# A gated mix of a state-space layer and a linear attention on one core: the last two output blocks scaled in halves on two engines, and the order of all steps written anew

## The chip, the cores and the metric

The kernel runs on one core of a Trainium2 chip. The metric is the device time of one execution in microseconds (us). The kernel before took 155.13 us, the median of three runs (154.61 to 155.14).

## The reference, cut to what matters

```
g = sigmoid((x * gate_w).sum(-1))                 # x: 2048 x 512, bf16
a = 2 * Re(C h_t) + x * Dskip,  h_t = Lam_bar * h_(t-1) + B_bar x_t     # 512 complex states
q, k, v = x @ wqkv in 32 heads of 16;  pq = q @ w_phi, pk = k @ w_phi
phi(p) = concat(softmax(p), softmax(-p));  kv = sum_s phi(pk) v^T;  z = sum_s phi(pk)
b = (phi(pq) kv / (phi(pq) z + 1e-6)) @ wo
out = g * a + (1 - g) * b
```

## The kernel before, in words

The 2048 rows are dealt into 8 residues of 256 rows; a block is 128 rows of one residue, so there are 16 blocks. Everything lies in on-chip memory; eight PSUM banks take the results of the matmuls. Each piece of work is a Python generator whose `yield`s cut it into segments. One long string, `ORDER`, is an order written out by hand or by a planner: each token runs the next segment of a step, and the instructions of each engine keep this order (a manual schedule), so the string alone decides who stands behind whom on TensorE, VectorE, ScalarE and on SyncE's DMA queue. In a token, `@5` gives the PSUM banks that a segment takes, `:D` sends an evacuation to VectorE (ScalarE otherwise) and `:A` sends an output DMA to ScalarE's queue (SyncE's otherwise).

The steps that the change and the prediction touch:

- `W`, `f`: the key weights are transposed and folded with `w_phi`. `l8` to `l15` load a block of x transposed (`xT`, L229; blocks 0 to 7 are loaded ahead of the list); `NR` and `NI` load B (L284); `R` transposes B by DMA into `BT` (L288); `C`, `Q` and `J` do likewise for C and the query weights.
- `k`, `v`, `q` (L475): four 128x512 matmuls per block and an evacuation. `V` and `V2` turn small vectors through TensorE. `P`, `U`, `M`, `D`, `i`: the tables of the state-space layer; `M` runs on GpSimd.
- `x`, `n`, `e`, `s` with a number: max, min, exponential and normalisation of the keys' features of one group; `xA` to `sA`, and `X1` to `S3`, the same for the queries' groups of four blocks. The last VectorE segment of `sA` and of `S1` to `S3` is the multiplication L559; behind it four DMA transposes write `phT` (L563).
- `a` (L578): accumulation of kv. `g` (L601): B x, and `z`: the scan over time. `h` (L668): states of the other residues; for five residues VectorE adds the two parts (L672). `c`: scaling of C.
- For block n: `y` (L717, L722) is the state-space output, accumulated in a bank `py`; `o` takes `phT` to `pn` (L736), then `ld` and `rd` on ScalarE, `nu` on either engine, `on` on VectorE (L744), and the transposed `oT`, by DMA (L758), or through TensorE for blocks 12 to 15 (L753); `t` adds `oT @ Wo` to `py` (L765), scales by the gate into `ot` (L769 on ScalarE, L771 on VectorE) and stores it (L773).

In the evacuation of `pn`, ScalarE reads the sums (`ld`) and one of the engines the rest (`nu`) of the same PSUM tile:

```python
            aexp(out=ld[:, hf], in_=pn[:, :, Dh], func=ACT.Ln)
            evac(nu[:, hf], pn[:, :, 0:Dh])
```

Of the kernel before, what the change touches and what calls it, by code (L numbers as in the profile page):

```python
# [23 lines left out]
ORDER = """
NR F:28 NI B W1@0 W0@1 W0 W2@2 W1:D W3@3 W3 f1@4 W2:D f0@5 f2@6 f0 f1:D l10 V@0 F:4 V P f3@1 f3 f2:D F:4 P P k1@2 k1
l13 P2 k0@3 P2 U P2 P2 P2 P2 P4 k2@4 P3 P3 k3@5 P4 P4 k0 v0@0 i0 i2 U i0 i0 i1 i2 k4@7 i0:D i0 k2 i2 i2:D i2 U k3 k5@6
i1 v3@1 n0 x0 l9 i1 V2@2 i3 l12 x0 k4 v2@3 i3 i3 l14 i1 k5 n0 x0 n0 x0 i3 k7@4 n0 x0 U n0 i1 l11 k6@5 n1 x1 x1 n1 x1
n1 l8 R0 R1 x1 i3 k7 M v7@7 x1 n1 n1 k6:D L V2 v1@6 x2 n2 e0 v6@4 v5@5 v4@2 e0 x2 s0 v0 l15 n2 s0 n2 v2 s0 v1 R2 s0 v6
v3 n2 k10@0 k10 s0 k9@3 k9 C4 k13@6 gw D R3 s0 k12@4 e1 v7 s0 e1 s1 C6 k11@1 k11 x2 s1 k14@0 k8@3 k12 k14 k8 v4 k13
a0@71 a0 x2 s1 x2 s1 v5 g00@4 g00 g60@0 n2 x3 s1 g20@3 g60 s1 g10@2 g10 n3 e2 g30@6 g40@5 g10 s1 a1 x3 g20 n3 a1 x3 n3  # L30
x3 g41@4 n3 C3 e2 e2 e2 x3 g30 g40 g30 k15@0 k15 n3 e3 s2 x4 s2 x4 g01@2 g01 e3 e3 s2 g50@3 g11@5 g50 s2 s2 s2 n4 x4
n4 Q3 n4 s2 g50 g21@6 e3 s3 v8@0 g31@2 g11 Q2 g11 n4 g70@3 Q1 s3 C7 g21 g70 v9@5 g70 g70 z0 z0 g31 g31 Q0 w1@6 C0 a2
a2 a2 w0@3 s3 z0 v11@2 v9 g61@5 g41 R4 z0 w1 v8 z0 z0 g61 s3 w2@4 s3 s3 a2 x4 z0 z0 g51@6 g51 x4 w2 C2 s3 w3@0 g51 v11
n4 R5 w3 g71@5 g71 g71 g71 z1 z1 g02@4 g02 g42@6 a3 a3 z0 z0 g42 w0 e4 e4 z1 z1 z1 g62@2 g12@0 q1@5 C1 h50@4 C5 J1 e4
e4 z1 q2@6 q2 g12 g12 g22@3 g22 J0 h50 z1 z1 g62 q3@4 q3 J2 s4 z1 s4 q0@6 z1 s4 q0 q1 xA nA g32@0 J3 g32 g32 h60@3 J0
g52@2 g52 c4 h60 J2 c4 g52 h51@4 c2 s4 s4 g72@6 R7 g72 xA h10@5 nA g72 g72 c2 xA J3 nA h10 v10@0 v10 J1 s4 c5 h51 c5
R6 g23@3 v12@2 c4 c0 c0 g63@5 nA z2 z2 a3 a3 g03@4 xA g03 z2 z2 z2 z2 xA g23 z2 z2 g33@6 c5 v12 z2 z2 g13@0 g13 g63
g43@4 h32@3 g13 nA g43 h52@2 h52 g33 h32 h61@5 h61 h12@0 c0 g53@4 h12 g33 g53 s4 v14@3 c2 eA eA h42@2 h42 g73@6 g53 eA
eA g73 g73 q10@5 sA h11@0 h11 O h00@4 g73 sA v13@2 h00 v13 a4 z3 sA v15@6 z3 v15 h20@0 h01@4 h30@2 v14 h20 sA h30 z3
h31@6 z3 z3 sA a4 h01 h31 c6 c6 sA q13@3 q13 z3 a4 a4 Y Y h22@0 G q10 z3 z3 G q6@2 q6 h22 z3 z3 sA sA Y Y c1 c1 q9@4  # L40
q8@6 q5@7 h62@3 h41@5 c3 h41 c1 c3 c3 h13@0 h62 q11@2 h13 q11 q8 q12@1 c6 q12 h21@5 q5 h21 h02@2 c7 q4@6 q4 h53@3 h53
h23@1 h23 h33@0 h33 sA q9 h40@7 h40 sA q7@5 h43@6 h63@3 c7 h43 q7 c7 y4@0 y4 sA h63 sA h03@1 END h02 o0@4 o0 X1 N1
o1@7 o1 q14@6 X1 N1 h03 o0@5 X1 o1@2 o1 o1 o0 o0 q15@3 o2@4 o2 o2@7 o2 N1 q15 X1 N1 X1 N1 E1 E1 y2@1 y1@2 y1 E1 E1 q14
X2 y0@5 y0 o1 y4 X2 N2 X2 o0 o0 o3@4 o3 o3@7 o3 o1 o3 y2 X2 N2 o2 X2 N2 S1 S1 N2 S1 o3 S1 N2 S1 S1 o3 y5@3 o2 o2 S1 S1
S1 y1 E2 E2 E2 E2 y9@6 G N3 y5 y5 y3@4 y2 X3 X3 N3 t1 G t1 N3 S1 N3 S2 y9 y9 S2 S2 S1 S1 S2 y3 y3 t3 y0 t0 t0 t2 t2
y6@7 X3 t2:A o4@2 o4 o4@5 o4 o4 y6 y6 t3 X3 o4 X3 o4 S2 S2 t3 o5@1 o5 o5@2 o5 o5 y13@5 y13 o5 N3 o6@4 S2 o6 o6@1 o6 o6
y12@2 o5 y7@4 y7 y12 o6 o6 t4 y7 S2 S2 t4:D S2 E3 E3 E3 E3 S2 o7@1 o7 t5 t5 S3 o7@0 o7 S3 o7 t6 S3 o7 S2 o7 y8@1 o8@3
t6 o8 o8@0 o8 o8 S3 S3 y12 t0:A y11@7 o8 o8 o9@3 o9:D o9@0 o9:D S3 y8 y8 o9 o9 S3 S3 o9 o10@3 y11 o10 o10@0 y11 o10
o10 S3 y14@3 S3 y14 t7 t7:D t8 y14 t8 y15@0 o11@4 S3 o11 o11@1 t9 o12@4 o11:D o11 S3 o10 o10 o12 o12@1 o12 o12 t9:D
o11 y15 o13@4 o13:D o13@6 t6:A o13 o13 o11 o12 y10@1 o14@4 y15 o14:D o12@6 t9 o12:D t7:A t1 y10 y10 o13 o15@4 o15  # L50
o15@6 t4:A t5 o15 o15 t8 o15 t12 t12 t12:A t10 o14@4 o14 o14 t10:D o13@6 t11 o15@2 o15 t10 o13:D t11 t11:A y13 t13 o14
o14@1 t15 t15 t15 o14:D t14 t13 t13 t14 t14:A
"""
# [15 lines left out]
def kernel(  # L69
# [691 lines left out]
    def st_t(n):  # L761
        ti = order[n]
        py, oT = live["py", n], live["oT", n]
        for g in range(HG):
            MM(out=py[:], lhsT=oT[:, g, :], rhs=Wo[:, g, :], start=False, stop=(g == HG - 1))  # L765
        yield
        ot = pools["op"][1].tile([P, D], BF16, name="ot", bufs=14)
        if sel["eng"] == "act":
            nc.scalar.mul(out=ot[:], in_=py[:], mul=G[:, ti:ti + 1])  # L769
        else:  # L770
            VS(out=ot[:], in0=py[:], scalar1=G[:, ti:ti + 1], scalar2=None, op0=ALU.mult)  # L771
# [76 lines left out]
```

## Time and profile before

| | |
|---|---|
| three runs | 154.61, 155.14, 155.13 us; median 155.13 |
| the profiled execution | 155.28 us, of which its span is 153.2 |
| busy in the span | TensorE 146.2 (95%), VectorE 132.4 (86%), ScalarE 129.2 (84%), GpSimd 15.8 us |
| granted TensorE clock | 0.995 |
| transfers | 17.55 MB by DMA, mean 115 GB/s |

The span runs from the first to the last instruction; 2.1 us lie around it. Durations of single instructions overlap on an engine, so sums of durations are larger than busy times.

### The profile page before, as it was taken

The numbers are of one execution on the slowest core, as the hardware profiler recorded it, in microseconds if no ns is written. First come the engines' busy times: TensorE is split into PE (matmuls) and PEld (weight loads), VectorE is DVE, ScalarE is ACT, GpSimd is POOL, SyncE is SP. The second block draws the span as 40 slices with busy tenths as digits, with TensorE's granted clock in tenths as the row PEclk, the third lists the DMA queues.
The fourth block names the chain that finished last, engine by engine and source line by source line (L and its number), as shares of the span: only waits on it lengthen the run. The fifth ranks groups of instructions, "written<-read, shape, count | busy, mean of one in ns | idle before, by whom it ended". The sixth has DMA issues, their size and how long they took to land.

```text
span 153.2 us, 3361 instructions
## 1 busy us (share of the span) xinstructions
PE 146.2 (95%) x1236; PEld 95.0 (62%) x1254; DVE 132.4 (86%) x303; ACT 129.2 (84%) x279; POOL 15.8 (10%) x43
## 2 busy tenths in 40 slices
PE   7899999999999999999999999999999999999990
PEld 7644434788878985869867656555554455555540
DVE  3799999999999999999999999999999958717520
ACT  3489998999998999999998999699498998627562
POOL 8239980000000000000000000000000000000000
PEclk9999999999999999999999999999999999999997
DMA  4875995534445699930000007711278859969842
GB/s 116 164 218 97 223 178 112 103 75 103 103 107 78 129 230 178 166 115 4 0 0 4 0 0 169 74 37 34 42 98 147 176 122 189 162 129 206 247 143 103
DMA packets 50848, 17.55 MB, mean 115 GB/s; under 512 B 44176, under 2 KB 50832, under 8 KB 50832
## 3 DMA queue, kind: packets, MB, share of 16 engines
q1 hardware_dynamic: 48976, 15.75, 53.8%
q10 hardware_dynamic: 1696, 1.57, 3.2%
q8 instruction: 10, 0.16, 0.5%
q0 software_dynamic: 160, 0.01, 0.2%
q14 instruction: 6, 0.05, 0.1%
HBM read 2.64 MB, written 2.10 MB: 31 GB/s over the span
## 4 chain that ended last, share of the span: by engine, by line
PE 78%; SPq 10%; DMA 7%; issue 1%; ACT 1%
PE pgq L601 18%; PE py L717 16%; PE pq L475 9%; PE py L765 8%; SPq L229 8%; PE pv L475 4%; PE ph L668 4%; PE pk L475 4%; DMA xT<-in_A_x_dram 4%; PE kvacc L578 3%; DMA phT<-EEq 3%; PE pn L736 3%; PE pgq L606 2%; PE py L722 2%; PE pgq L608 2%; SPq L284 1%
## 5 line engine op out<-in xcount | busy, mean ns | idle before, releaser
L601 PE MATMUL pgq<-xT,BT 128*128 128x256 bf16 x256 | 31.5, 272 | 0.0
L475 PEld LDWEIGHTS <-xT 128*128 128x128 bf16 x192 | 18.2, 98 | 18.3 <-DMA xT<-in_A_x_dram 0.7
L601 PEld LDWEIGHTS <-BT 128*128 128x128 bf16 x256 | 24.6, 98 | 4.1
L138 ACT ACTIVATE EEk<-EEk 128x1024 bf16<-128x1024 bf16 x20 | 20.4, 1080 | 0.0
L119 ACT CAST uv<-pgq 128x512 bf16<-128x512 f32 x28 | 15.9, 605 | 0.5 <-PE pgq L601 0.4
L475 PE MATMUL pv<-Wv,xT 128*128 128x512 bf16 x59 | 15.5, 379 | 0.3
L475 PE MATMUL pq<-Wq,xT 128*128 128x512 bf16 x60 | 15.4, 379 | 0.2
L765 PE MATMUL py<-Wo,oT 128*128 128x512 bf16 x62 | 15.3, 379 | 0.1
L475 PE MATMUL pk<-Wk,xT 128*128 128x512 bf16 x62 | 14.7, 379 | 0.3 <-DMA xT<-in_A_x_dram 0.2
L138 ACT ACTIVATE EEq<-EEq 128x1024 bf16<-128x1024 bf16 x12 | 11.7, 1042 | 0.3 <-DVE EEq L527 0.3
L769 ACT ACTIVATE ot<-py,G 128x512 bf16<-128x512 f32 x12 | 7.9, 686 | 4.5 <-PE py L765 4.3
L138 ACT ACTIVATE ld<-pn 128x16 f32<-128x16 f32 x32 | 6.1, 191 | 5.7 <-PE pn L736 4.6
L590 ACT ACTIVATE phT<-X,dgB 128x512 bf16<-128x512 bf16 x16 | 10.7, 725 | 0.0
L119 ACT CAST nu<-pn 128x256 bf16<-128x256 f32 x27 | 9.9, 380 | 0.0
L119 ACT CAST vx<-pv 128x512 bf16<-128x512 f32 x16 | 9.1, 604 | 0.4 <-PE pv L475 0.4
L548 DVE TENSOR_TENSOR EEk<-EEk,rck 128x4096 bf16<-128x4096 bf16 (+1 forms) x5 | 9.3, 1858 | 0.0
L744 DVE TENSOR_TENSOR on<-nu,rd 128x512 bf16<-128x512 bf16 x16 | 6.7, 421 | 2.8 <-ACT rd L138 1.6
L765 PEld LDWEIGHTS <-oT 128*128 128x128 bf16 x64 | 5.7, 97 | 5.3 <-DMA oT<-on 0.5
L119 ACT CAST Xq<-pq 128x512 bf16<-128x512 f32 x16 | 8.9, 608 | 0.0
L119 ACT CAST Xq<-pk 128x512 bf16<-128x512 f32 x15 | 8.6, 598 | 0.4 <-PE pk L475 0.4
L736 PEld LDWEIGHTS <-phT 128*128 128x128 bf16 x128 | 6.2, 97 | 3.8 <-DMA phT<-EEq 1.4
L511 DVE TENSOR_TENSOR smk<-smk 128x512 bf16<-128x512 bf16 (+4 forms) x18 | 8.1, 448 | 0.1
(178 smaller groups left out, 321.2 us busy)
## 6 DMA issues: line engine op xcount, KB each, us to landing
X<-HM SPq DMA_DIRECT2D x8, 256.0 KB, 4.5
out_dram<-ot ACTq DMA_DIRECT2D x8, 128.0 KB, 2.5
out_dram<-ot SPq DMA_DIRECT2D x8, 128.0 KB, 2.2
C2r<-in_B_wqkv_dram ACTq DMA_DIRECT2D x2, 256.0 KB, 3.8
Wv<-in_B_wqkv_dram SPq DMA_DIRECT2D x1, 512.0 KB, 4.0
Bn<-in_A_B_re_dram SPq DMA_DIRECT2D x1, 512.0 KB, 5.7
Bn<-in_A_B_im_dram SPq DMA_DIRECT2D x1, 512.0 KB, 6.8
Wo<-in_B_wo_dram SPq DMA_DIRECT2D x1, 512.0 KB, 4.3
```

The source lines that it names most:

```text
L119: nc.scalar.copy(out=out_ap, in_=in_ap)
L138: ins = nc.scalar.activation(**kw)
L229: nc.sync.dma_start_transpose(out=xT[:, :, ti * P:(ti + 1) * P], in_=x_res[ti // 2, ti % 2])
L475: MM(out=pt[:], lhsT=xT[:, kt, ti * P:(ti + 1) * P], rhs=W[:, kt, :], start=(kt == 0), stop=(kt == KT - 1))
L511: VT(out=dst, in0=cur[:, :, :, 0:n, :], in1=cur[:, :, :, n:2 * n, :], op=op)
L548: VT(out=E5, in0=E5, in1=rc.to_broadcast([P, L, 2 * NB, Dh, 4]), op=ALU.mult)
L590: nc.scalar.mul(out=t_, in_=x_, mul=c_)
L601: MM(out=pg[:, h, :], lhsT=BT[:, kt, 2 * j + h, :], rhs=xT[:, kt, r * NC:(r + 1) * NC], start=(h == 0 and kt == 0), stop=(r % 2 == 0 and k ...
L717: MM(out=py[:], lhsT=hs(r, t, slice(a * P, (a + 1) * P)), rhs=C2B[t], start=(t == 0), stop=False)
L736: MM(out=pn[:, 4 * m:4 * m + 4, :].rearrange("p h e -> p (h e)"), lhsT=ph[:, 4 * hf + m, :], rhs=KVm[:, 4 * hf + m, :], start=(m == 0), st ...
L765: MM(out=py[:], lhsT=oT[:, g, :], rhs=Wo[:, g, :], start=False, stop=(g == HG - 1))
L769: nc.scalar.mul(out=ot[:], in_=py[:], mul=G[:, ti:ti + 1])
```

## The change

In `st_t` the last two blocks of the order of outputs (n = 14 and 15) are no longer scaled by one instruction over 512 columns. ScalarE scales columns 0 to 255 and VectorE columns 256 to 511, of the same PSUM tile `py` into the same tile `ot`; one DMA stores both. The string `ORDER` is replaced as a whole. It has the same 855 tokens; their order, the banks and the letters for engines and queues differ. The diff, with the ORDER lines that the prediction speaks of:

```diff
 ORDER = """
-NR F:28 NI B W1@0 W0@1 W0 W2@2 W1:D W3@3 W3 f1@4 W2:D f0@5 f2@6 f0 f1:D l10 V@0 F:4 V P f3@1 f3 f2:D F:4 P P k1@2 k1
-l13 P2 k0@3 P2 U P2 P2 P2 P2 P4 k2@4 P3 P3 k3@5 P4 P4 k0 v0@0 i0 i2 U i0 i0 i1 i2 k4@7 i0:D i0 k2 i2 i2:D i2 U k3 k5@6
-i1 v3@1 n0 x0 l9 i1 V2@2 i3 l12 x0 k4 v2@3 i3 i3 l14 i1 k5 n0 x0 n0 x0 i3 k7@4 n0 x0 U n0 i1 l11 k6@5 n1 x1 x1 n1 x1
-n1 l8 R0 R1 x1 i3 k7 M v7@7 x1 n1 n1 k6:D L V2 v1@6 x2 n2 e0 v6@4 v5@5 v4@2 e0 x2 s0 v0 l15 n2 s0 n2 v2 s0 v1 R2 s0 v6
...
-o11 y15 o13@4 o13:D o13@6 t6:A o13 o13 o11 o12 y10@1 o14@4 y15 o14:D o12@6 t9 o12:D t7:A t1 y10 y10 o13 o15@4 o15
-o15@6 t4:A t5 o15 o15 t8 o15 t12 t12 t12:A t10 o14@4 o14 o14 t10:D o13@6 t11 o15@2 o15 t10 o13:D t11 t11:A y13 t13 o14
-o14@1 t15 t15 t15 o14:D t14 t13 t13 t14 t14:A
+NR l8 B F:28 W1@0 NI W1 W0@1 W2@2 W2:D W3@3 l13 f1@4 W0 f0@5 W3 f0 f2@6 f1:D V@0 V l9 f2:D F:4 P P f3@2 U P2 f3 U P P2
+P2 P2 U P2 P4 P4 F:4 U k0@1 k0 V2@3 P3 k3@4 V2 P2 P3 k1@0 P4 k1 k2@5 i0 i1 i0 i0 i0 k2 i0 i1 v2@7 i2 i2 i2 k3 n0 x0 gw
+x0 n0 k4@6 i2 k4 x0 i1 i1:D i3 i3 k5@2 k5 n0 i3 x0 n0 v4@1 x0 l11 i3:D v3@3 n0 x1 n1 v6@0 l14 M x1 i1 i2 i3 L n1 x1 n1
+x1 n1 k7@5 x1 l10 l12 n1 k6@4 k6:D v5@6 k7 n2 x2 e0 e0 v0@2 v0 s0 s0 x2 s0 R0 n2 v2 v6 v1@5 v1 e1 k8@4 x2 k8 s0 s0 n2
+v7@2 v7 D v3 k13@7 k13 s0 e1 s0 R1 k9@0 v5 s1 n2 R3 s1 k14@5 k14 k11@4 k11 k10@2 k10 x2 C7 k12@3 k9 l15 R2 k12 C3 v4
...
+q11@7 q11 G q8 h22 h41@0 h43@3 h41 q14@4 sA sA h03 h20@2 h43 q14 h20 c7 sA sA h63@7 h63 END X1 N1 X1 o0@0 o0 q15@6 q15
...
+t12:D o15 o15 o15 o14@6 o14 t1 o14 t10 t10 o14 o13@2 t10:A t11 o15@6 o15 t12 o13:D o14@3 t13 t11 t11 y15 t15 y14 t13
+o14:D t15 t13:A t15 t14 t14 t14
 """
...
         ot = pools["op"][1].tile([P, D], BF16, name="ot", bufs=14)
-        if sel["eng"] == "act":
+        if n >= NTI - 2:
+            nc.scalar.mul(out=ot[:, 0:D // 2], in_=py[:, 0:D // 2], mul=G[:, ti:ti + 1])
+            VS(out=ot[:, D // 2:D], in0=py[:, D // 2:D], scalar1=G[:, ti:ti + 1], scalar2=None, op0=ALU.mult)
+        elif sel["eng"] == "act":
             nc.scalar.mul(out=ot[:], in_=py[:], mul=G[:, ti:ti + 1])
```

More of the change, by code (lines that the diff above doesn't have):

```diff
@@ L24 @@
 ORDER = """
-NR F:28 NI B W1@0 W0@1 W0 W2@2 W1:D W3@3 W3 f1@4 W2:D f0@5 f2@6 f0 f1:D l10 V@0 F:4 V P f3@1 f3 f2:D F:4 P P k1@2 k1
-l13 P2 k0@3 P2 U P2 P2 P2 P2 P4 k2@4 P3 P3 k3@5 P4 P4 k0 v0@0 i0 i2 U i0 i0 i1 i2 k4@7 i0:D i0 k2 i2 i2:D i2 U k3 k5@6
-i1 v3@1 n0 x0 l9 i1 V2@2 i3 l12 x0 k4 v2@3 i3 i3 l14 i1 k5 n0 x0 n0 x0 i3 k7@4 n0 x0 U n0 i1 l11 k6@5 n1 x1 x1 n1 x1
-n1 l8 R0 R1 x1 i3 k7 M v7@7 x1 n1 n1 k6:D L V2 v1@6 x2 n2 e0 v6@4 v5@5 v4@2 e0 x2 s0 v0 l15 n2 s0 n2 v2 s0 v1 R2 s0 v6
-v3 n2 k10@0 k10 s0 k9@3 k9 C4 k13@6 gw D R3 s0 k12@4 e1 v7 s0 e1 s1 C6 k11@1 k11 x2 s1 k14@0 k8@3 k12 k14 k8 v4 k13
@@ L30 @@
[L30 to L49, printed above, removed]
@@ new lines @@
+x0 n0 k4@6 i2 k4 x0 i1 i1:D i3 i3 k5@2 k5 n0 i3 x0 n0 v4@1 x0 l11 i3:D v3@3 n0 x1 n1 v6@0 l14 M x1 i1 i2 i3 L n1 x1 n1
+x1 n1 k7@5 x1 l10 l12 n1 k6@4 k6:D v5@6 k7 n2 x2 e0 e0 v0@2 v0 s0 s0 x2 s0 R0 n2 v2 v6 v1@5 v1 e1 k8@4 x2 k8 s0 s0 n2
+v7@2 v7 D v3 k13@7 k13 s0 e1 s0 R1 k9@0 v5 s1 n2 R3 s1 k14@5 k14 k11@4 k11 k10@2 k10 x2 C7 k12@3 k9 l15 R2 k12 C3 v4
+a0@76 a0 Q2 g00@5 s1 g60@4 g00 x2 g20@2 s1 s1 g40@0 R5 g60 g10@3 s1 n2 e2 e2 g40 e2 g10 x3 k15@1 s1 a1 e2 n3 a1 g21@5
+R4 g01@4 x3 g20 C2 k15 Q0 v9@0 n3 x3 n3 x3 n3 g10 g30@2 g30 x3 g21 g01 n3 g31@1 e3 g50@3 e3 Q1 Q3 g11@5 g11 s2 s2 s2
@@ new lines @@
+x4 g30 g50 C4 s2 n4 s2 s2 e3 x4 g41@4 g50 g70@2 g70 e3 g11 n4 g70 g41 g70 x4 g02@3 C1 s2 a2 a2 v9 s3 w0@5 n4 s3 x4 g02
+a2 a2 s3 v8@4 z0 s3 v8 O w0 z0 w2@2 w2 n4 g22@0 g22 g31 g31 z0 z0 z0 z0 s3 w1@3 w1 x4 g61@4 g61 z0 n4 z0 C5 g51@5 s3
+s3 R7 g51 g51 w3@2 w3 e4 z0 z0 g71@0 g71 g71 g71 q3@1 g12@3 g12 g12 C6 q3 e4 z1 z1 C0 e4 e4 z1 q2@4 z1 z1 z1 q1@5 J3
+h50@2 h50 g42@0 z1 z1 g42 g32@3 g32 g32 q2 J2 s4 J1 q0@1 q1 z1 z1 h10@2 g62@0 g62 J0 c2 J0 h60@3 h60 h10 J2 s4 g52@4
+q0 nA g52 g52 xA h51@5 g72@0 nA h30@3 c4 g72 v10@1 c4 c4 s4 xA v11@2 g72 g72 z2 c5 v10 z2 J1 h51 v11 R6 g23@4 g63@0 nA
@@ new lines @@
+J3 z2 g43@1 z2 z2 c0 h30 z2 nA g23 a3 z2 z2 c0 xA g43 c5 g03@5 g03 s4 s4 s4 h61@2 a3 z2 a3 a3 xA g13@3 g13 g13 z2
+h32@4 g33@1 h12@5 g33 h32 g63 h42@3 h52@4 xA c2 g33 g53@0 g53 nA eA eA eA c5 g73@1 g53 h12 q9@5 h61 h11@2 h52 h42 eA
+c0 v13@4 v13 g73 s4 g73 g73 sA v14@3 c3 h11 v15@0 v15 v12@4 v12 q4@2 q4 sA q12@1 h62@0 z3 z3 sA z3 v14 c2 c1 z3 c1 sA
+sA h62 z3 z3 a4 a4 h31@4 h31 h02@2 h02 q10@3 q10 c1 a4 a4 z3 z3 sA sA Y q5@0 z3 G c6 Y c6 z3 q7@4 Y q7 Y h00@2 h00 sA
+q6@3 c6 q9 h13@7 h13 q8@6 h53@4 h53 c3 h22@2 h33@5 q6 q12 c3 h40@7 h40 h21@3 h33 h21 q5 h03@1 h23@4 h23 c7 c7 h01@5
@@ new lines @@
+q11@7 q11 G q8 h22 h41@0 h43@3 h41 q14@4 sA sA h03 h20@2 h43 q14 h20 c7 sA sA h63@7 h63 END X1 N1 X1 o0@0 o0 q15@6 q15
+y2@3 y6@1 N1 o1@4 X1 o1 o2@2 o2 o0@0 o1@7 o0 o0 o1 o2@6 N1 X1 y2 y2 h01 N1 o2 X1 y3@4 N1 X2 N2 y3 X2 o1 E1 E1 E1 o0 X2
+o1 X2 o0 N2 E1 X2 N2 o1 S1 o3@2 o3 o3@0 y5@7 y5 o3 y5 S1 o3 o3 S1 N2 y0@5 y0 S1 y9@6 N2 y9 q13@2 S1 S1 o2 o2 G o3 q13
+S1 S1 o2 y3 E2 X3 y1@0 y1 y1 E2 E2 t1 S1 S1 S1 S1 X3 y4@2 G N3 y0 t0 N3 N3 t3 X3 E2 S2 S2 X3 t1 t0 y4 t2 t2 y13@0 t0:A
+S2 o4@5 o4 o4@3 S2 y6 y6 N3 o4 o4 o5@5 o4 t3 o5 o5@3 o5 X3 y13 o5 o5 o4 S2 y4 S2 o6@4 o6 o6@5 o6 N3 y12@3 t3 y12 o6 o6
@@ new lines @@
+y7@4 t4 S2 E3 o5 S2 o7@5 t4:D o6 E3 E3 y7 y7 E3 S3 S3 y9 o7 o7@2 o7 o7 o7 S2 S2 S2 S2 t5 t5 t6 o7 t6 y8@5 S3 o8@2 y12
+S3 o8 o8@7 o8 o8 o8 S3 S3 o8 y11@1 o9@2 o9:D o9@7 o9 o9 t2:A y8 y8 o9 o9 y13 o10@7 S3 o10:D o10@2 y11 o10 y14@7 y14 S3
+S3 S3 S3 o11@2 S3 o11:D t7 t7:D o10 o10 o10 t8 t8:D o11@2 o11 o11 t9 t9 o11 o11 t5 y15@4 o12@2 o12:D t9 o12@5 o12 o12
+o12 t7 t6:A y11 y15 o13@6 o13:D t8 o13@2 o13 y10@5 o14@6 o14:D o12@2 o12 y10 t4 y10 o15@6 o15:D o15@2 o13 o13 t12
+t12:D o15 o15 o15 o14@6 o14 t1 o14 t10 t10 o14 o13@2 t10:A t11 o15@6 o15 t12 o13:D o14@3 t13 t11 t11 y15 t15 y14 t13
```

## Prediction, made before the changed kernel ran

> **What bounds the kernel now.** I first read the busy time by stages (the windows view: length, then busy us and instruction counts of PE, PEld, DVE, ACT, POOL, then clock, DMA share and GB/s).
>
> ```profile
> 5.00:10.00 5.00, 4.66 (x49) 3.11 (x48) 4.12 (x18) 3.80 (x8) 0.62 (x3) 1.00 0.69 170
> 10.00:113.00 103.00, 102.25 (x874) 69.37 (x884) 102.15 (x224) 96.66 (x193) 11.01 (x26) 1.00 0.49 92
> 113.00:143.00 30.00, 29.55 (x244) 15.98 (x247) 21.18 (x42) 22.09 (x67) 0.00 (x0) 1.00 0.90 163
> 143.00:153.00 10.00, 6.12 (x43) 3.17 (x42) 2.79 (x6) 5.41 (x14) 0.00 (x0) 0.93 0.49 158
> ```
>
> From 10 to 113 us TensorE is idle for 0.75 us and VectorE for 0.85: both are full. From 113 to 143 TensorE is full with 0.45 idle, and the SyncE queue (timeline) issues almost without a pause:
>
> ```profile
> 109.73 3.20 SPq L758 DMA_TRANSPOSE oT<-on  x2
> 113.03 6.66 SPq L563 DMA_TRANSPOSE phT<-EEq  x4
> ...
> 124.61 5.39 SPq L563 DMA_TRANSPOSE phT<-EEq  x4
> 130.10 4.62 SPq L758 DMA_TRANSPOSE oT<-on  x3
> 134.83 5.39 SPq L563 DMA_TRANSPOSE phT<-EEq  x4
> 140.31 2.57 SPq L758 DMA_TRANSPOSE oT<-on  x2
> ```
>
> So three limits run side by side: VectorE's work up to the multiplication L559 of S1, which opens the transposes at 113.03; SyncE's row of transposes from there to 142.9; TensorE throughout. Where TensorE waited is in the chain of waits, with the end of the kernel:
>
> ```profile
> 17.02 5.82 DMA xT<-in_A_x_dram
> 22.89 5.35 PE pk L475 x24
> ...
> 116.71 4.37 DMA phT<-EEq
> 121.13 0.43 PE pn L736 x8
> ...
> 147.44 0.88 PE py L765 x4
> 148.34 0.89 ACT ot L769 x2
> 149.23 0.27 issue
> 149.50 0.69 ACT ot L769
> ```
>
> The reader sees a block of x that landed at 22.84, just as TensorE needed it, a phT that landed at 121.09, and a tail: TensorE's last group ends at about 149.2, ScalarE is busy with t15 and t13 until then and starts t14 at 149.50, 0.3 late; the store is issued at 150.22.
>
> **The two halves.** Prices come from the groups by shape (count, then busy us and mean ns of one):
>
> ```profile
> L769 ACT ACTIVATE ot<-py,G 128x512 bf16<-128x512 f32 x12 | 7.9, 686 | 4.5 <-PE py L765 4.3
> ...
> L771 DVE TENSOR_SCALAR ot<-py,G 128x512 bf16<-128x512 f32 x4 | 3.0, 750 | 4.2 <-PE py L765 4.1
> ...
> L121 DVE CAST nu<-pn 128x256 bf16<-128x256 f32 x5 | 2.0, 423 | 2.6 <-ACT ld L138 2.6
> ```
>
> The old price is the 686 ns of an `ot` of 512 columns on ScalarE, plus the 0.3 that it queued. A half on ScalarE: a 256-column copy from PSUM takes 356 to 428 ns (`nu`, L119), and scaling costs 686 - 605 = 81 ns over a copy of 512 columns (`vx`, `uv`), so about 0.45. On VectorE: `nu` 423 ns, scaling 750 - 685 = 65 over a copy of 512 (L121), so 0.49. Side by side they would end 0.49 after the matmuls.
>
> But they do not run side by side. In the instruction order of the changed kernel VectorE's half of t14 waits for one thing, ScalarE's counter at the value of ScalarE's own half; it has no wait on TensorE. The trace of before has the same pattern wherever two engines read one PSUM tile: `nu` on VectorE waits for `ld` on ScalarE (waits view: us in all, times, longest).
>
> ```profile
> DVE nu L121 <- ACT ld L138: 2.6, 3, 1.9
> ```
>
> [...]
>
> So the halves come in a row: TensorE ends at 149.17, ScalarE starts at 149.20 (t13 now stands ahead of y15's and t15's last matmuls, so the queue of 0.3 is gone), 0.45 to 149.65, a hand-over of 0.04, 0.49 to 150.18. The old instruction ended at 149.50 + 0.69 = 150.18 as well. Gain 0.0 us. Bounds: -0.5 if they did overlap, +0.3 if ScalarE is not free in time. For the latter: behind t15's half ScalarE issues t13's store (0.34); 0.45 + 0.34 fit into the 1.08 that TensorE needs for y14's last four (0.22) and t14 (0.86). t15's VectorE half holds up nothing but t14's. The store of t14 moves from ScalarE's queue to SyncE's (0.34 against 0.33). Three more stores are SyncE's; they stand behind its last transpose, where seven stores took 0.33 to 0.57 each, so all are through before t15.
>
> **The new order: what stays.** TensorE has the same matmuls. On VectorE I counted what stands ahead of S1's L559 in both lists: 228 segments each. Only before: W1's copy (0.43), now ScalarE's, and two of the tables' absolute values (0.29) against two others; only after, a G of 0.17. W1's copy ran at 5.1 us, when VectorE had idle time (4.12 busy in 5 us), so it opens nothing. An instruction right behind its own predecessor in a tree starts later: a 512-column step is followed after 0.34 us by independent work and after 0.45 by its successor. Such pairs fall from 15 to 13: 2 x 0.115 = -0.2 us. SyncE's row from o0 to o11 has the same transposes in the same order: 0.
>
> **What moves.** (a) x blocks. k0 starts at 7.67 as k1 did: W, f, V and the fillers stand alike, and V still waits for its DMA. From there TensorE's needs follow by counting: four matmuls of 512 take 0.864 (16 take 3.45). Ahead of k8 stand 15 such groups and V2 (0.1): needed at 20.7. l8 goes into NI's slot, 13.7; with the longest latency of an x block, 6.7, it lands at 20.4. k9 is needed at 23.3 and its slot is the old one, landed 22.84; k13 is needed at 22.5, against 15.7 + 6.7 = 22.4. So the wait of 0.33 at 22.3 goes. Bounds -0.33 and +0.3. NI is one slot later, which R0 at 24.4 still covers. (b) l15 is issued at about 29.6, k15 needed at 33.1; latencies of 2.8 to 4.1 give 32.4 to 33.7: 0 to +0.6, I take +0.2. (a) and (b) cancel nearly, and both lie on TensorE, where the later phT wait hides what is won. (c) U, V2 and gw come early on VectorE, among operations of 0.2 us. V2's selection (L320, 0.97 us) now stands ahead of M on GpSimd; it fits in before M's `dl` products, which began at 10.9, and if it does not, D covers it: M ended at 21.7 and D began at 24.2. 0. (d) The additions L672 at the end of the states: adding up each queue's traced durations in its new order, I estimate that VectorE now reaches those of h20, h40 and h41 0.2 to 0.3 us before their matmuls end; in the trace the closest (h43) ran 0.2 after. This is a new wait on VectorE, with X1, S1 and all transposes behind it: +0.2, bounds 0 and +1.2. (e) The phT wait at 120.6 (0.35) stays: same row of transposes, o6 at the same sum.
>
> **Sum.** On the path that sets the end: tail 0.0, dependent pairs -0.2, additions +0.2, so 0 against the profiled 155.28. That execution stands 0.15 above the median of the runs, so I forecast 155.1.
>
> **Rivals.**
> 1. *Gain.* The 0.33, the 0.35 and the 0.2 all come off, and no new wait appears: 155.13 - 0.9 = 154.2. For it: the list avoids the known late block. Against it: SyncE's row ends at 142.9 whatever TensorE does, and t11 needs an oT that landed at 144.3, with 4.3 us of matmuls behind it, so without an earlier S1 no more than 0.35 can come off. 0.16.
> 2. *Halves overlap*: 155.1 - 0.5 = 154.6. Against it stands the wait. 0.03.
> 3. *Slower: VectorE waits for the states.* It decides if TensorE is over 0.7 us late at h20 (about 96 us): then VectorE, which has no slack until 113, waits, and S1's transposes and the end move one for one. Two evacuations of 0.6 that free a bank late are enough: 155.1 + 1.2 = 156.3. For it: the list packs producers and users closer than the old one, and a full VectorE cannot recover anything. Against it: under the old list, as tight elsewhere, VectorE lost 0.85 us in 103. 0.24.
> 4. *Slower: x late.* l8, l13 and l15 late by 0.3, 0.3 and 0.6, passed on through the keys to VectorE: 156.3. 0.12.
>
> **How the numbers follow.** The case of no net change has 0.45, and with rival 2 gives 0.48 for within 0.5% (154.4 to 155.9), about what a measurement of this kernel can tell from no change. Faster 0.16, slower 0.24 + 0.12 = 0.36. The range goes from rival 1's edge, 154.3, to 156.7, which leaves out the worst of rivals 3 and 4. The likeliest case's own range is 154.6 to 155.6.
>
> **What would show it.** Right: `ot` of 256 columns on VectorE starts where ScalarE's ends; the last store is issued 1.0 us after TensorE's end; the x wait is gone; the phT transposes start near 113.0; span near 153.1. Wrong: the two `ot` overlap; L672 has idle time on `ph` of over 0.5; the first phT of S1 is issued over 0.5 us away from 113.0; TensorE has new waits for xT or for a bank.

## The result, and the profile after

The changed kernel takes 156.91 us (median of six runs, 156.44 to 157.72) beside 155.45 for the kernel before (six runs, 154.61 to 156.58): a ratio of 1.0103, with a 95% interval of 1.0070 to 1.0135, so some 1.6 us slower. The profiled execution took 156.62 us with a span of 154.5, against 155.28 and 153.2. The forecast was 155.1, with a range up to 156.7.

The stages, in the windows view of the changed kernel (length, then busy us and counts of PE, PEld, DVE, ACT, POOL, then clock, DMA share, GB/s):

```profile
10.00:113.00 103.00, 101.89 (x872) 69.49 (x881) 101.84 (x219) 96.69 (x193) 7.93 (x26) 1.00 0.49 92
113.00:143.00 30.00, 28.05 (x228) 15.30 (x231) 21.31 (x42) 21.50 (x65) 0.00 (x0) 1.00 0.94 158
```

Up to 113 us TensorE is idle for 1.11 us (0.75 before) and VectorE for 1.16 (0.85). Between 113 and 143 TensorE's idle time goes from 0.45 to 1.95: that is where the time went. SyncE's row of transposes, in the timeline of the changed kernel (start, us):

```profile
113.38 6.63 SPq L563 DMA_TRANSPOSE phT<-EEq  x4
...
125.06 5.41 SPq L563 DMA_TRANSPOSE phT<-EEq  x4
130.57 4.75 SPq L758 DMA_TRANSPOSE oT<-on  x3
135.49 5.38 SPq L563 DMA_TRANSPOSE phT<-EEq  x4
140.96 2.54 SPq L758 DMA_TRANSPOSE oT<-on  x2
```

It runs 0.35 to 0.72 later than before from its first instruction on (113.38 against 113.03 at its start, 135.49 against 134.83 for S3's transposes). The chain of waits that ended last begins in this row:

```profile
130.57 5.68 DMA oT<-on
136.25 0.05 issue
136.30 0.82 PE py L765 x3
...
149.76 0.88 PE py L765 x4
150.64 0.02 issue
150.66 0.48 ACT ot L769
151.15 0.02 issue
151.17 0.48 DVE ot L770
```

o7's transposes, issued at 130.57, landed after 5.68 us, and t7's matmuls waited for them from 134.65 to 136.25. Before, they were issued at 130.10 and landed at 134.46, after 4.36 us, and TensorE came to them at 134.70: it had 0.24 us to spare. Behind that the chain is TensorE without a gap, and then the two halves one behind the other. The waits of the changed kernel (us in all, times, longest):

```profile
PEld L765 <- DMA oT<-on: 1.6, 1, 1.6
PEld L475 <- DMA xT<-in_A_x_dram: 1.1, 3, 0.7
DVE mc L628 <- ACT va L119: 0.3, 1, 0.3
DVE ot L770 <- ACT ot L769: 2.6, 2, 2.0
```

The first line is the wait of t7. The second is mostly k15, which stood 0.80 us from 33.0 on for block l15 (issued 29.65, landed 33.57); the wait for a block at 22.3 is gone. The third is a new wait of VectorE, at 66.7: the scan's first product `mc` waits for ScalarE's four copies `va` of g72. The fourth is the halves.

Two theories stood at the start. A: the store of t2, which the new list issues on ScalarE's queue at 130.82, just behind o7's transposes, stretched them; before, the store nearest to them (t0's) was issued at 129.70, ahead of them. B: the row is late because VectorE is late, and everything behind S1 follows. The expectations below name the rivals of A by letters of their own.

### The profile page after: what moved, and what is told of

Read it like the earlier page. It is cut to its first block, busy times and chain, and to the rows that moved or that the text cites. A ratio compares the mean times of both kernels' runs of the same rounds, so it can differ in the third digit from the quotient of the medians.

```text
span 154.5 us, 3364 instructions
## 1 busy us (share of the span) xinstructions
PE 145.7 (94%) x1237; PEld 95.2 (62%) x1254; DVE 133.2 (86%) x305; ACT 129.5 (84%) x279; POOL 13.1 (8%) x43
## 5 line engine op out<-in xcount | busy, mean ns | idle before, releaser
L765 PE MATMUL py<-Wo,oT 128*128 128x512 bf16 x62 | 15.6, 379 | 1.6 <-DMA oT<-on 1.5
L119 ACT CAST uv<-pgq 128x512 bf16<-128x512 f32 x28 | 16.5, 609 | 0.3 <-PE pgq L601 0.2
L475 PE MATMUL pv<-Wv,xT 128*128 128x512 bf16 x61 | 15.0, 379 | 0.2
L590 ACT ACTIVATE phT<-X,dgB 128x512 bf16<-128x512 bf16 x16 | 11.3, 732 | 0.1
L765 PEld LDWEIGHTS <-oT 128*128 128x128 bf16 x64 | 5.7, 98 | 6.5 <-DMA oT<-on 1.6
L119 ACT CAST nu<-pn 128x256 bf16<-128x256 f32 x25 | 9.3, 390 | 0.0
L736 PE MATMUL pn<-KVm,phT 128*128 128x68 bf16 x128 | 7.2, 194 | 0.2 <-DMA phT<-EEq 0.2
```

The source lines that it names most:

```text
L119: nc.scalar.copy(out=out_ap, in_=in_ap)
L475: MM(out=pt[:], lhsT=xT[:, kt, ti * P:(ti + 1) * P], rhs=W[:, kt, :], start=(kt == 0), stop=(kt == KT - 1))
L590: nc.scalar.mul(out=t_, in_=x_, mul=c_)
L736: MM(out=pn[:, 4 * m:4 * m + 4, :].rearrange("p h e -> p (h e)"), lhsT=ph[:, 4 * hf + m, :], rhs=KVm[:, 4 * hf + m, :], start=(m == 0), st ...
```

## The halves by themselves

**The kernel before with the halves.** The edit is that of `st_t` alone; the old list stays.

> The kernel before, with the scaling of t15 and t14 in halves as the only edit; the step list is the old one. Theory of the prediction (the halves come one behind the other): a half on ScalarE of 0.45 to 0.48 us, then one on VectorE of 0.48 behind it, against one whole output of 0.69 that had queued 0.3 on ScalarE: 0.0, bounds -0.1 to +0.3, so 155.3 to 155.7 beside a run of before at 155.4. Rival (the halves overlap, or VectorE's starts on the matmuls' end alone): -0.3 to -0.5, so about 155.0. The trace tells it directly: VectorE's half of t14 starts where ScalarE's ends, or beside it.

Measured: 157.00 us beside 155.53, ratio 1.0103 (1.0059 to 1.0148). The timeline of this kernel at its end (VectorE's line shows its idle time and what ended it):

```profile
148.34 0.48 DVE L770 TENSOR_SCALAR ot<-py,G 128x256 bf16<-128x256 f32 x1 [2.53 <-ACT ot L769]
148.74 0.41 DVE L121 COPY oT<-po 128x512 bf16<-128x512 bf16 x1
149.21 0.55 PEld L765 LDWEIGHTS <-oT 128*128 128x128 bf16 x4 [1.91 <-DVE oT L121]
```

t15's half on VectorE waits for ScalarE's half, and in the old list the copy of o14's transposes from PSUM (L121) stands behind it on VectorE. TensorE's last group waits 1.42 us for that copy. This profile is of the fastest of the six executions, 155.90 us; the others took 156.1 to 158.0. The halves need the copy ahead of them, as the new list has it.

**The same, with o14's copy ahead.**

```diff
-o14@1 t15 t15 t15 o14:D t14 t13 t13 t14 t14:A
+o14@1 t15 o14:D t15 t15 t14 t13 t13 t14 t14:A
```

> The kernel before with the halves, as in the first run of that, where t15's half on VectorE stood ahead of the copy of o14's transposes from PSUM and so held up t14's matmuls by 1.4. Here that copy (o14:D) is moved ahead of t15's scaling, as the changed kernel's list has it. If the halves in themselves are worth 0.0 (bounds -0.1 to +0.3): 155.4 to 155.8, no wait for oT ahead of t14's matmuls, and 1.04 to 1.06 us from TensorE's end to the last store's issue, as in before. If the halves cost something by themselves, it stays near 156.5.

Measured: 155.91 beside 155.39, ratio 1.0017 (0.9989 to 1.0044). TensorE ends at 149.94 and the last store is issued at 151.08, 1.14 us later (1.05 before; ScalarE still has t13's output in hand). The profile also has a wait of 0.85 for o8's transposes, of the kind treated below.

**The changed kernel with whole outputs.**

```diff
-        if n >= NTI - 2:
-            nc.scalar.mul(out=ot[:, 0:D // 2], ...)
-            VS(out=ot[:, D // 2:D], ...)
-        elif sel["eng"] == "act":
+        if sel["eng"] == "act":
```

> The changed kernel's step list, with the outputs of t15 and t14 scaled whole on ScalarE as before. If the halves cost time under this list (TensorE ended at 150.64, a whole output of 0.69 would end 151.35, the two halves ended 151.65), it is 0.3 faster than the changed kernel: 156.6 where that is 156.9, still over 1 us above before. If the halves carry the whole loss, it comes back to 155.4. If they help, it is slower than the changed kernel. The wait for the transpose of o7 (1.6 us at 134.7 in the changed kernel) stays as it is by every theory.

Measured: 156.89, ratio to before 1.0077 (1.0045 to 1.0109), where the changed kernel has 1.0103. So the halves cost between nothing and some 0.4 us; the loss stays without them. This kernel's profile shows more of another cause. Its waits of VectorE ahead of 113 us begin with

```profile
DVE EEk L521 <- PE kvacc L578: 0.9, 1, 0.9
```

l15 landed at 34.06 here, k15 waited 1.16 us, the accumulation behind k15 on TensorE came late, and VectorE's L521 stood for it. In the changed kernel's own profile the same gap was 0.10.

## The store behind o7's transposes

**t2's store later on ScalarE's queue.**

```diff
-... o9@7 o9 o9 t2:A y8 y8 ...     -... t7 t6:A y11 ...
+... o9@7 o9 o9 y8 y8 ...          +... t7 t6:A t2:A y11 ...
```

> The changed kernel, with the store of t2 moved from behind o9's segments (issued 130.82, just behind the two transposes of o7 that were issued at 130.57) to right behind the store of t6, some 6 us later. Theory A (the store's packets get in between the transposes' and stretch them): o7's transposes land after 4.4 us as in the kernel before instead of 5.7, TensorE's wait of 1.6 us at 134.7 falls to 0.3 or less, and the time falls by 1.0 to 1.4 us to 155.5 to 155.9. Theory B (the instruction fetches of 8 and 16 KB at 131.7 and 134.4 stretch them): the latency stays over 5.2, the wait over 1.2, and the time at 156.5 to 156.9.

Measured: 159.65, ratio 1.0272 (1.0219 to 1.0325). Theory A's first half held: o7's transposes landed after 4.46 us and TensorE's wait fell to 0.50. But the new place made a worse wait, in ScalarE's timeline of this kernel:

```profile
140.11 3.80 ACTq L776 DMA_DIRECT2D out_dram<-ot  x2
143.95 0.26 ACT L138 ACTIVATE ld<-pn 128x16 f32<-128x16 f32 x2 [3.89 <-DMA phT<-EEq]
```

In the traces of before and after the 95 transfers of SyncE and ScalarE use eight semaphores in turn, in the order of the list, and none of the 87 that have a predecessor on their semaphore was issued before that one had landed; the closest, a store of ScalarE in before, was issued at 143.10, 0.02 us after a landing at 143.08. For t2's store this was now S3's fourth transpose, which landed at 143.55; the store was issued at 143.57, and ScalarE's queue stood with `ld` behind it.

**t2's store on SyncE's queue behind the row.**

```diff
-... o9@7 o9 o9 t2:A y8 y8 ...     -... o13:D t8 o13@2 ...
+... o9@7 o9 o9 y8 y8 ...          +... o13:D t8 t2 o13@2 ...
```

> The changed kernel, with the store of t2 taken off ScalarE's queue (issued 130.82, just behind o7's transposes) and put on SyncE's queue behind the row of transposes, as the sixth of the stores there, where nothing waits for it. Theory A (that store's packets stretch the transposes that are in flight): o7's latency goes from 5.7 to about 4.4 as in the run with t2's store later (4.46), TensorE's wait at 134.7 from 1.6 to about 0.5, and, without that run's block of ScalarE (a store there waited 3.1 us for a transpose that shared its semaphore), the end comes 1.0 earlier: a span near 153.5 and 155.7 to 156.0. Theory B (the landing of o7 sets nothing behind it, because SyncE's row and the last transposes end where they did): the wait goes, and comes back in the stretch behind 138 us, the time stays at 156.6 to 156.9.

Measured: 156.69, ratio 1.0082 (1.0054 to 1.0110): 0.2 below the changed kernel, the number of the second theory in the expectation. o7 took 4.51 us and TensorE waited 0.70 for it. The waits of TensorE's weight loads behind 113 us show where the rest went:

```profile
PEld L736 <- DMA phT<-EEq: 2.4, 6, 0.7
PEld L765 <- DMA oT<-on: 0.7, 1, 0.7
```

TensorE, which waits 0.9 less there, now stands for the S3 transposes that follow in the same row, 0.33 at 141.7 and 0.32 at 143.5; in the changed kernel the weight loads' wait for phT was 0.7, once.

**The reverse on the kernel before.**

```diff
-... S3 S3 y12 t0:A y11@7 o8 o8 o9@3 o9:D o9@0 ...
+... S3 S3 y12 y11@7 o8 o8 o9@3 o9:D t0:A o9@0 ...
```

> The reverse on the kernel before: its store of t0 on ScalarE's queue, issued at 129.70, 0.4 ahead of o7's transposes (130.10), goes two tokens later, to about 130.5, just behind them. Nothing else is moved. Theory A: o7's latency rises from 4.36 to about 5.5 and TensorE waits 0.8 to 1.1 for it at 134.7, which is 0.24 before that landing now; the time rises by 0.5 to 1.1 to 156.0 to 156.6. Theory C (o7 is late in the changed kernel for another reason, such as its instruction fetches at 131.7 and 134.4, and t2's store had only the packets left over): latency and time stay within 0.2 of before.

Measured: 156.48 beside 155.39, ratio 1.0066 (1.0041 to 1.0092). The store was issued at 130.57, 0.52 behind o7's transposes instead of 0.40 ahead, and the chain of waits of this kernel reads

```profile
130.05 5.70 DMA oT<-on
135.79 1.90 PE py L765 x8
```

o7's latency went from 4.36 to 5.70 and TensorE waited 1.15 us. This is theory A by itself: one store, moved by 0.9 us, costs 1.0 us (0.6 to 1.4 by the interval). In this run a store on ScalarE's queue, issued 0.52 us behind transposes on SyncE's, went with 1.3 us more of their latency; how packets of the two queues share the transfer time, no trace here shows.

**The three stores out of the row, on the kernel before.**

```diff
-... y6@7 X3 t2:A o4@2 ...   -... S2 S2 t3 o5@1 ...   -... y12 t0:A y11@7 ...   -... t7:A t1 y10 ...
+... y6@7 X3 o4@2 ...        +... S2 S2 o5@1 ...      +... y12 y11@7 ...        +... t7:A t1 t0 t3 t2 y10 ...
```

> The kernel before, with its three stores that are issued among the row of transposes (t2 at 117.5 and t0 at 129.7 on ScalarE's queue, t3 at 121.6 on SyncE's) moved to SyncE's queue behind the row. Where a store in flight beside transposes stretches them, those of S1 and of o7 land earlier (4.4 us now, 3.3 to 3.8 then), the wait for phT at 120.6 (0.35) goes, and SyncE's row gains the 0.35 of t3's issue: a gain of 0.2 to 0.6, 154.8 to 155.2. If only a store behind a transpose that TensorE is about to need costs anything, the time stays within 0.2 of before.

Measured: 156.46, ratio 1.0055 (1.0031 to 1.0079): slower, against both expectations. S1's third and fourth transposes did land sooner (3.3 us instead of 4.4 and 3.7), the wait at 120.6 went, and the row ran some 0.7 ahead: o7's, issued at 129.39, landed in 2.51. But now o8's, issued at 130.73, took 4.75 with no store in flight, and t8 waited 0.63. And a store on ScalarE's queue stood for the store that had used its semaphore (landed 144.85, issued 144.87), with 0.86 us of TensorE behind it.

So transposes issued near 130 to 131 us landed late in both lists, store or not (4.36 us before, 5.68 in the changed kernel, 4.75 here). The transfers view in quarters of a microsecond from 128 to 138 shows what else goes on there (GB/s, 40 slices), first before, then changed:

```profile
GB/s 205 175 131 216 208 212 185 139 212 224 198 210 215 335 225 219 201 105 74 191 197 51 12 11 9 12 8 160 216 141 0 0 158 224 206 209 182 119 208 214
```

```profile
GB/s 210 207 206 154 163 205 214 212 178 127 217 217 200 216 195 151 177 163 77 27 8 9 60 305 236 265 122 8 7 24 110 293 115 0 28 213 212 217 194 167
```

In both kernels the transfers nearly stop for some slices, at 8 to 27 GB/s (133.5 to 134.75 before, 132.75 to 133.5 changed), and the changed kernel has a second such stretch from 134.75 to 135.5. In the packets this goes with instruction fetches: one packet of 16 KB that takes 1.23 us (from 132.44 before, 131.72 changed), and one of 8 KB (132.63 before, 134.37 changed). Before, 13 short packets of the transposes that began at 133.2 to 133.4 took 1.05 to 1.22 us each, where the median packet of the 4 us ahead takes 0.018; all 13 ended at 134.43 or 134.44, 0.77 us after the 16 KB packet, and o7's transposes landed at 134.46. The changed kernel has two such groups. In the first, which ends at 133.7, 14 of the 16 packets are those of t2's store; the second, of the transposes' packets, ends at 135.65, 1.0 us after the 8 KB packet. o7's transposes landed at 136.25 there, 0.6 us later, where before it was 0.02 to 0.03 us after the held packets. That a few held packets hold up a whole transpose is the author's reading of these times.

In all 20 profiles such a group of 11 to 24 held packets ends 0.76 to 1.00 us after each of the two 16 KB fetches beside the row of transposes. o7's transposes landed 0.8 to 1.6 us after the end of a fetch in 18 of the profiles; in the other two (2.5 and 2.8 us) they had landed before the 16 KB packet was through. A store behind them adds to that, but not every time: with a store issued 0.1 to 0.6 us behind, o7's took 5.4 to 5.7 us in six profiles of eight and 4.4 and 4.8 in two; without one, 4.2 to 4.8 in the ten profiles where the fetch caught them. One of these ten bears on the run with t0's store behind o7, where the 8 KB fetch also came later (133.25 to 134.70): with the halves and o14's copy ahead it fell at the same time (133.13 to 134.71) and no store stood behind o7, which took 4.58. That the fetches are the cause is inferred from these times. A kernel without them was not tried, and similar groups stand at 60 to 65 us in 18 of the profiles with no fetch near.

## The late block and VectorE

**l15 one slot earlier.**

```diff
-... k10@2 k10 x2 C7 k12@3 k9 l15 R2 ...
+... k10@2 k10 x2 l15 C7 k12@3 k9 R2 ...
```

> The changed kernel, with the load l15 of the last block of x moved ahead of C7 in the step list, some 1.3 us earlier. The wait of k15 for it (0.8 us at 32.9) goes down to 0.1 or less by every theory. If TensorE's lateness there is passed on through the keys and the states to S1's first transposes (113.4 against 113.0 in before), these come 0.3 to 0.5 earlier, o7's transposes land in time or nearly, and the time falls by 0.4 to 1.5. If what is won there is lost again behind VectorE and the row of transposes, the first transposes of S1 stay within 0.1 of 113.4 and the time within 0.2 of 156.9.

Measured: 156.59, ratio 1.0070 (1.0044 to 1.0096), 0.3 below the changed kernel. The wait of k15 went. TensorE, 0.8 earlier, then waited 0.81 at 45.7 for an `HM` that took 4.33 us to land, and S1's first transpose was issued at 113.58, no earlier.

**Three moves together.** l15 as above, t2's store on SyncE's queue as above, and t6's store later:

```diff
-... o12 t7 t6:A y11 y15 ...   -... o14:D o12@2 o12 y10 t4 ...
+... o12 t7 y11 y15 ...        +... o14:D o12@2 o12 t6:A y10 t4 ...
```

> The changed kernel with three moves together: t2's store on SyncE's queue behind the transposes, t6's store on ScalarE's queue some 2 us later (it follows S3's fourth transpose by 1.0 and stretched it from 3.3 to 4.2 in the run with l15 early), and l15 one slot earlier. If the stores among the transposes and the late x block are the whole loss, 155.2 to 155.6, level with before. If something else in the new list costs (the row of transposes starting 0.35 to 0.45 late), 155.6 to 156.0. If it beats before by over 0.3, the list as such is better than the old one and only these three places were wrong in it.

Measured: 158.02, ratio 1.0161 (1.0127 to 1.0196). S3's fourth transpose landed in 3.30 instead of the 4.21 with l15 alone, as meant, but t6's store stood on ScalarE's queue for o11's transposes, which had its semaphore (landed 145.19, issued 145.21), and TensorE lost 1.78 us behind it. The sum of the three moves is not measured by this run.

**One more instruction on VectorE, kernel before.** The first step of the minimum tree of the second query group is done twice, to the same result.

```diff
             VT(out=dst, in0=cur[:, :, :, 0:n, :], in1=cur[:, :, :, n:2 * n, :], op=op)
+            if key == ("mn", "G1") and n == Dh // 2:
+                VT(out=dst, in0=cur[:, :, :, 0:n, :], in1=cur[:, :, :, n:2 * n, :], op=op)
```

> The kernel before with one more instruction on VectorE: the first step of the minimum tree of the second group of queries (128x1024, 0.6 from start to start) is done twice, to the same result, ahead of S1. It measures by itself what a later start of the row of transposes is worth under the old list: in four profiles of the old list S1's first transpose was issued at 112.86 to 113.03, in six of the new one at 113.38 to 113.86, a difference of 0.65 between the means. Theory R (VectorE has no slack and the row of transposes behind it sets the end): the first transpose moves to 113.5 to 113.7 and the time rises by 0.4 to 0.8, to 155.8 to 156.2. Theory S (there is slack in the row, and only the store behind o7 costs): the first transpose moves, the time stays within 0.2 of before.

Measured: 155.82 beside 155.50, ratio 1.0019 (0.9993 to 1.0044). S1's first transpose moved from 113.03 to 113.78, and the time by some 0.3 (-0.1 to 0.7 by the interval). The profile shows another victim: o7's transposes, issued at 130.90, still took 4.28, but o3's, issued at 112.48, were now caught by the fetch at 114.80 and took 4.31 instead of 2.48, and TensorE waited 0.8 us for them at 116.0. By the median, more than half of the lateness is lost under the old tail.

**VectorE's two waits taken away, changed kernel.**

```diff
-... g10 x3 k15@1 s1 a1 e2 n3 a1 g21@5 R4 ...   -... g72 g72 z2 c5 v10 z2 J1 h51 v11 ...
+... g10 x3 s1 a1 e2 n3 a1 g21@5 k15@1 R4 ...   +... g72 g72 h51 c5 v10 z2 z2 J1 v11 ...
```

> The changed kernel, with two edits in the step list that take VectorE's two new waits away and leave all transfers where they are: k15 goes behind a1 and g21 on TensorE, so that the late block l15 holds up neither a1's matmuls nor, through them, VectorE's L521 (0.1 to 0.9 us at 35.3 to 35.8 in the profiles of the new list); and the addition of h51 (L672, 0.69) goes ahead of z2's first two products, of which the first waited 0.25 to 0.37 for ScalarE's copies of g72. Theory R: S1's first transpose comes 0.3 to 0.6 earlier than the 113.6 of the new list, at 113.0 to 113.3, and the time falls by 0.3 to 0.8 to 156.1 to 156.5. Theory S: it stays at 156.6 to 156.9.

> The same two edits for VectorE, and the stores of t2 and t6 taken from ScalarE's queue among the transposes and put on SyncE's queue behind the row. If VectorE's two waits and the stores among the transposes are together what the new list loses, 155.2 to 155.7, level with before. If only the sum of one of them comes back, 156.1 to 156.5. Below 155.0 it would be a version that beats both.

Measured: 163.67 and 162.39, ratios 1.0493 (1.0453 to 1.0533) and 1.0433 (1.0402 to 1.0465). Neither tests the theory: h51's addition now stood ahead of J1 in the list, so J1's transfer of `HM` waited for it, in SyncE's waits of the first of the two

```profile
SPq L301 <- DVE HM L672: 9.5, 1, 9.5
```

and the transposes of `BT` behind it in the queue came 4.5 us late for TensorE. A token moved past a transfer of the same tile moves the transfer.

**The same with J1 kept ahead.**

```diff
-... g72 g72 z2 c5 v10 z2 J1 h51 v11 ...
+... g72 g72 J1 h51 c5 v10 z2 z2 v11 ...
```

> The changed kernel, with k15 behind a1 and g21 on TensorE and h51's addition ahead of z2's products on VectorE, this time behind J1, so that J1's transfer waits for nothing new. The waits of VectorE for g72's copies (0.25 to 0.37 at 66.8) and for the keys behind k15 (0.1 to 0.9 at 35.3) go; S1's first transpose comes 0.3 to 0.6 earlier than 113.6. By the run with 0.6 more on VectorE (0.3 for 0.75) that is worth 0.1 to 0.3 of time: 156.6 to 156.8. If the head's lateness is the loss, 155.6 to 156.2.

Measured: 156.85 beside 155.57, ratio 1.0069 (1.0036 to 1.0102), at most a few tenths below the changed kernel. Both waits are gone, but `mc` of an earlier scan (0.25 at 46.8) and a step of the keys' sum (0.21 at 80.0) wait instead; S1's first transpose is issued at 113.29.

## Head against tail

**New list up to END, old list behind it**, and **old list up to END, new list behind it**. A few tokens were fitted (named in the expectations); the first has whole outputs, the second the halves.

> A step list made of the new list up to END and the old list from there on, with the outputs scaled whole as before. Four tokens had to be fitted: q13 and h01 stand where the old tail had q14 and h03, and y4's first two segments follow o1. If the loss sits in the new list's tail (the store behind o7, TensorE's needs against the row of transposes), it is within 0.3 of before: 155.2 to 155.8. If it sits in the head (VectorE's new waits, S1's first transpose 0.65 later), 156.2 to 156.9.

> The reverse: the old list up to END and the new list from there on, with the halves. Fitted: q14 and h03 for q13 and h01, and y4 left to the tail. If the loss sits in the tail, 156.4 to 157.0 although S1's first transposes come at the old list's 112.9 to 113.1. If it sits in the head, 155.3 to 155.9.

> The old head with the new tail, and t2's store taken from behind o7's transposes to SyncE's queue behind the row. If that store is the tail's loss, it falls back to 155.4 to 155.9 here, where the row starts in time, while the same edit under the new head brought 0.2 only. If the tail loses by its order too, it stays over 156.2.

Measured, all beside 155.57: new head with old tail 157.31, ratio 1.0102 (1.0066 to 1.0139); old head with new tail 156.17, ratio 1.0025 (0.9991 to 1.0059); the same without t2's store in the row 156.09, ratio 1.0021 (0.9988 to 1.0054). By the second hybrid the larger part of the loss comes with the new list's head, some 0.8% of the 1.0%. The first adds little to that: at its seam TensorE waits 1.9 us between 97 and 100 us, which neither list has, for PSUM banks that ScalarE's copies and one of VectorE's additions L672 free late (they end at 97.87, 98.87 and 100.18, and the matmuls of `pn` start 0.04 later). In the second the tail is the changed kernel's, t2's store included, but the row starts at 112.90, o7's latency is 4.44 although t2's store is issued 0.61 behind it, and t7 does not wait.

**One more instruction on VectorE, old head with new tail.** The edit of the run on the kernel before, on the second hybrid.

> The old head with the new tail (156.17, 0.25% over before), and the first step of the second query group's minimum tree done twice on VectorE ahead of S1, as in the run on the old list, where it moved S1's first transpose by 0.75 and cost 0.3. If the new tail is bound by the row of transposes that VectorE opens, the first transpose moves from 112.9 to 113.6 and the time rises by 0.6 to 0.8, to 156.7 to 157.0: the changed kernel's time, with the old head. If the new tail has the same slack as the old one, it rises by 0.2 to 0.4, and the head loses by something else than VectorE's lateness.

Measured: 157.09 beside 155.92, ratio 1.0072 (1.0048 to 1.0096). Set against 1.0025 without the instruction, that is 0.47%, some 0.7 us for 0.7 us on VectorE, where the old tail took 0.3. By the two intervals the 0.7 can be anything from 0.1 to 1.4 us, so the times alone do not tell the two tails apart, and the profile has to carry it. SyncE's row in this kernel's timeline, and TensorE's wait for o7 (two added lines make L565, L760 and L767 of L563, L758 and L765):

```profile
113.88 6.50 SPq L565 DMA_TRANSPOSE phT<-EEq  x4
...
130.91 5.27 SPq L760 DMA_TRANSPOSE oT<-on  x3
```

```profile
PEld L767 <- DMA oT<-on: 1.5, 1, 1.5
```

o7's transposes took 5.74 us, t2's store 5.04, S2's fourth transpose 5.06, and TensorE waited 1.5 us: the changed kernel's picture (5.68, 5.06, 4.76 and 1.6), made from the old head by making VectorE 0.7 late. Without the store behind o7, the same lateness in the old tail left o7's at 4.28.

**l9 ahead of l13, kernel before.**

```diff
-l13 P2 k0@3 ...   -... x0 l9 i1 V2@2 ...
+l9 P2 k0@3 ...    +... x0 l13 i1 V2@2 ...
```

> The kernel before, with the loads l9 and l13 of two blocks of x in each other's slot: l9, which k9 waits for at 22.3 (0.33 in the profile of before, 0.5 to 0.9 in the other profiles of the old list), goes to 15.7 and lands at about 22.3, l13, needed one product later, lands at 22.8. Nothing else moves. If the old list is bound by TensorE, 0.2 to 0.5 come off: 155.0 to 155.3. If what TensorE wins is lost again at the next wait for a phT (0.35 at 120.6), it stays within 0.2 of before.

Measured: 155.42 beside 155.92, ratio 0.9974 (0.9946 to 1.0002). The one wait that the new list did take away can be had in the old list for nothing; this is the fastest version of the study, some 0.4 us below before, just short of certain. In this profile o7's transposes, issued 130.17, landed in 2.81, before the stretch without transfers, where before, issued 130.10, they took 4.36.

## Why the prediction was wrong

The forecast of no change failed; the sign and nearly the size were rival 3's (156.3), with its place right (VectorE late, S1's transposes and the end behind it) and its mechanism wrong: VectorE did not wait for the states. Rival 4's way, l15 late and passed on through the keys to VectorE, is in the traces too (0.1 to 0.9 us of VectorE's time, 0.10 in the changed kernel's own profile).

- *The two halves: 0.0.* Right. VectorE's half starts 0.03 behind ScalarE's end, and the last store is issued 1.04 behind TensorE's end, as foreseen. The hand-over of 0.04 in the prediction is that of before, where `nu` on VectorE started at 140.25 and `ld` on ScalarE had ended at 140.21. That the halves could not overlap was not shown: in the changed kernel's profile VectorE waited for ScalarE both times (2.6 us in all), and no run tests halves without that wait. Alone, with o14's copy ahead, they cost 0.17% (-0.11 to +0.44). That t15's half on VectorE holds up nothing holds for the new list only.
- *What stays, SyncE's row: "the same transposes in the same order: 0".* This is the term that failed. The order was the same; the start was not (113.38 in the changed kernel's profile, 113.29 to 113.89 in seven other profiles of the new head, those with h51 ahead of J1 left out, against 112.75 to 113.16 in the eight of the old head without an added instruction), nor were the latencies (o7's 5.68 against 4.36). The prediction priced issue and order; it took a transpose's latency as given, and did not look at what else is in flight in those microseconds, though o7's 4.36 beside the 2.4 to 2.6 of its neighbours (the seven ahead of it from 105 us on) stood in the trace of before, with 0.24 us of margin behind it.
- *What stays, dependent pairs: -0.2.* Not seen. From the copy of the small vectors (`vec`, at 7.10 in both) to S1's L559, VectorE took 104.65 us before, of which 1.17 idle, and 104.99 after, of which 1.41 idle. Without idle time that is 103.48 and 103.58, and the new list has one more instruction there, worth 0.13.
- *What moves, (a) the blocks of x: -0.33 to +0.3.* Right: the wait at 22.3 went. *(b) l15: +0.2, hidden by the later phT wait.* The lateness was 0.8 (0.7 to 1.5 in the profiles of the new head with l15 in its slot), and it was not hidden: through the accumulation behind k15 it reached VectorE's L521, with 0.1 to 0.9.
- *What moves, (d) the additions L672: +0.2, up to 1.2.* The wait was not there at all. Another was, which was not looked for: `mc` for the copies of g72, 0.25 to 0.37 in every profile of the new head with that order. Together S1's first transpose, behind VectorE's L559, came 0.3 to 0.9 later in these profiles than in that of before; the terms for VectorE added up to 0.
- *(e) The phT wait stays at 0.35.* The size held by luck: the wait of 0.40 ends at 118.25 and is for S1's first transpose (4.83 us), while the wait at 120.6, for the third, is gone.
- *The sum* lacked a second price for lateness. It added what reaches VectorE and let it pass one for one; by the medians 0.75 costs 0.3 under the old tail and about all under the new one. The profiles give a reason: there t2's store stands behind o7, and TensorE's next needs stand right at the row's landings (o7 at 134.65; S3's at 141.7 and 143.5 once o7's wait is shortened).

How much of the head's part is the late l15, how much `mc`, and how much lies in the time at which the instruction fetches fall is not settled: each edit that took one of them away let the next wait step in. Nor does any run account for the 0.25% that may remain with the old head and the new tail (its interval includes none).

## What to carry to other kernels

A row of transposes with no pause is a clock: price the moment its first instruction is released (0.35 us late here, and 0.35 to 0.72 along the row), not only its order, and read each landing's margin against the engine that needs it (0.24 us for o7's). A transfer that took twice as long as its neighbours is a warning even where nobody waited for it; here a shift of the row by some 0.7 us put another one there, o8's (4.75 us) when it went ahead and o3's (4.31) when it came late. Before a store is moved to a free queue, look at which transfers will be in flight with it (1.3 us more for o7's here), and at which earlier transfer holds its semaphore (1.5 to 3.1 us of ScalarE here).

## What the runs showed of the hardware

- Transposes that take 2.4 to 2.6 us (`oT`) or 3.2 to 3.4 (`phT`) undisturbed mostly take 4.2 to 5.3 when an instruction fetch of 16 KB falls into them, and 5.4 to 5.7 in six profiles of eight where a store of 128 KB was issued 0.1 to 0.6 us behind them on another queue.
- Packets held in such a stretch end together, 0.76 to 1.00 us after the 16 KB packet, 40 times in 20 profiles. Stores feel it too: those issued at 144.84 and 145.51 before, ahead of the fetch at 146.06, took 3.9 and 3.5 us, and the one issued at 147.38, as it ended, 2.0.
- Whether a transpose is caught is a matter of a tenth: issued at 130.10 it took 4.36, issued at 130.17, with the fetch 0.1 later as well (132.54 against 132.44), it took 2.81.
- In three runs a store that ScalarE issues waited for its semaphore's last user, and ScalarE stood with it: 3.1, 2.0 and 1.5 us, each time until 0.02 us after the landing.
